# FFT filter and PReLU MLP on one core: the inverse transform's middle array laid out the other way, table and filter loads reordered

## The chip, the cores and the metric

The kernel runs on one core of a Trainium2 chip. The metric is the device time of one execution in microseconds; lower is better. Before the change the median of three runs is 773.36 us.

## The reference

Two computations follow each other. First each of 8 batches of 3008 positions by 256 channels is filtered in the frequency domain along the positions; then all 24064 rows go through a two-layer MLP whose activation has a learned slope for negative values.

```
X = np.fft.rfft(x, axis=1)                      # x: (8, 3008, 256)
Y = X * (filt_r + 1j * filt_i)[None]
y = np.fft.irfft(Y, n=3008, axis=1).reshape(24064, 256)
h = y @ w_in                                    # (256, 2048)
g = np.maximum(h, 0) + alpha * np.minimum(h, 0)
out = g @ w_out                                 # (2048, 256)
```

All inputs and the output are float32. The kernel works in float16 with float32 accumulation.

## The kernel before

**The transform.** 3008 = 94 x 32, so a transform over the positions is done as matrix products: a 94-point transform (stage a), a turn of the array, a 32-point transform with the twiddle factors folded into its tables (piece_b), the product with the filter, then the inverse 32-point transform (piece_c), a second turn, and the inverse 94-point transform (`inverse`), whose result goes to yT, the transposed input of the MLP.

**Batch 0 and the others.** Batches 1 to 7 turn their arrays through DRAM (a_dram, v_dram), hidden beside the MLP of earlier batches. Batch 0 has nothing to hide behind. Its class `First` keeps everything on the chip: it turns by matmuls with the identity matrix `id16` as the moving operand and the array as the weights. The change touches only batch 0's code, the order of loads around it, and the first MLP block.

**Batch 0 in order.** (1) Eight pieces `piece_a` (L322): 94-point transform of 4 of the 32 columns each, evicted to `am`; pieces 0 to 5 are evicted whole by ACT or DVE in turn, pieces 6 and 7 half by ACT and half by DVE (L336). Between them stand `warm` matmuls (L436), which compute nothing that is used. (2) `turn_at` (L338) turns `am` into `at`, two or four of 24 rows at a time. (3) Twelve steps kp: `piece_b(kp)` (matmuls L355, then on DVE the product with the filter, L360, into uu) and `piece_c(kp)` (L363, matmuls L382). PE issues piece_b(kp+2) ahead of piece_c(kp). `piece_c` uses two tables, twi_s and its swapped and sign-scaled copy twx_s; the two halves e=0 and e=1 of the array's rows run at the same time and go to different accumulator tiles. After every second kp `keep_c` (L386) evicts two tiles with ACT into `v` (seen as `vm`). (4) The second turn: `turn` (L393), by `half_t` (two of the 32 columns s, both channel halves) and `piece_t` (four). Its weights are 96 elements of `vm`. (5) `half_d` and `pair_d`: the inverse 94-point transform (L283, constants wi3_s) of four or eight columns, evicted to yT.

In `vm` an element's place is given by (g, m, e), where the column is s = 4g + e and m is the row; a weight load of one column therefore takes every fourth element:

```
m = self.vm.rearrange("p (g m e) -> p g m e", m=96, e=4)                     # L394
nc.tensor.matmul(..., m[:, 8 * f + s // 4, :, s % 4], id16, ...)             # L399
```

**Tables, filter and constants.** The forward table twf_s comes in three parts of 8 of 24 rows (`table`, L416, on SP's DMA queue). A memset on DVE ahead of parts 2 and 3 (L445, L453) holds each load back until DVE has come to that place. `inverse_table` (L419) turns each part into twi_s, and `swapped` (L426) makes twx_s from it, for rows 0 to 7 on DVE, for the others on POOL. The filter comes in three parts of eight DMAs each, issued by POOL (`load_filt`, L132, L140), after the eight loads of x. POOL's DMAs use eight semaphores in turn, so each issue waits until the eighth one before it has landed.

**After batch 0.** The first MLP block (512 rows) runs in halves of 256 rows: `up4` (L563) takes four of the 16 hidden groups, with two accumulating matmuls each (kt = 0 and 1, the two channel halves, L569). Its first call also issues two evictions of the second turn (`later`) and the transposed slopes. From then on a plan written out by hand (`put`, `plan_fft`) lays the pieces of the other batches between the MLP's matmuls; the order of each engine is fixed. In that plan batch 0 still has half_t(6) and (7) at step 3, piece_t(2) at step 1, piece_t(4), (5) at steps 19 and 23, piece_t(6), (7) at 32 and 34, with their pair_d after them.

**Pools.** psH has two tiles of two PSUM banks (hps), psF one of two banks, psO two of one bank (op). `bank("o")`, `bank("h")` and `bank("f")` take one bank from them.

Of the kernel before, what the change touches and what calls it, by code (L numbers as in the profile page):

```python
# [14 lines left out]
N1 = 94  # L15
# [10 lines left out]
def _build_consts():  # L26

    n1, n2, p = np.arange(N1), np.arange(N2), np.arange(32)
    k1 = (2 * (np.arange(NK) // 2) + 24 * (np.arange(NK) % 2))[None, :] + np.arange(2)[:, None]
    k2 = np.where(p < 16, p, 47 - p)  # L30
    g = np.where(p < 16, 1.0, -1.0)

    a1 = 2 * np.pi * n1[:, None, None] * k1[None] / N1
    wf1 = np.stack([np.cos(a1), -np.sin(a1)], axis=2)
    scale = np.where((k1 == 0) | (k1 == 47), 1.0, 2.0)[None, :, None, :] / NFFT
    wi3 = (wf1 * scale).reshape(N1, 96).T
    wfx = wf1.transpose(0, 3, 1, 2).reshape(N1, 96)
# [10 lines left out]
    return wf1, wfx, wfq, wi3, twf  # L48


@with_exitstack
def kernel(
# [8 lines left out]
    out: bass.AP,  # L61
):
    nc = tc.nc
    names = ("wf1", "wfx", "wfq", "wi3", "twf")
# [22 lines left out]
    wfq_s = konst.tile([128, 64], FP16, name="wfq_s")  # L87
    wfx_s = konst.tile([N1, 96], FP16, name="wfx_s")
    wi3_s = konst.tile([96, N1], FP16, name="wi3_s")
    twf_s = konst.tile([128, NK, 64], FP16, name="twf_s")  # L90
    twi_s = konst.tile([128, NK, 64], FP16, name="twi_s")
    filt_s = konst.tile([128, 12, 2, D], FP16, name="filt_s")
# [66 lines left out]
    class Fft:  # L159
        def __init__(self, b):  # L160
            self.b = b
            self.base = (b % 2) * NFFT
            self.uw = {}

        def start_a(self):
# [114 lines left out]
        def inverse(self, pd, g, dh, mh):  # L280
            ps = pd[:, 0 : 4 * N1].rearrange("p (m x) -> p m x", m=4)
            for m in range(4):
                nc.tensor.matmul(ps[:, m], self.zt[:, 8 * g + 4 * mh + m, dh * 128 : dh * 128 + 128],  # L283
                                 wi3_s, start=True, stop=True)
            return ps

        def half_d(self, i, evict, kind, fill=0):
# [19 lines left out]
    def on_dve(o, i):  # L307
        nc.vector.tensor_copy(o, i)  # L308
# [4 lines left out]
    class First(Fft):  # L313
# [7 lines left out]

        def piece_a(self, i, wide):  # L322
            c, sh = i // 2, i % 2
            ps = banks(wide)
            for f in range(2):
                for u in range(4):
                    o = (4 * sh + u) * D + 128 * f
                    nc.tensor.matmul(ps[:, f, 96 * u : 96 * u + 96], xc[(0, c)][0:N1, o : o + 128], wfx_s,
                                     start=True, stop=True)
            o = self.am.rearrange("p (f m s) -> p f m s", f=2, s=N2)[:, :, :, 4 * i : 4 * i + 4]  # L330
            s = ps[:, :, 0:384].rearrange("p f (s m) -> p f m s", s=4)
            if i < 6:
                both[i % 2](o, s)
            else:
                for f in range(2):
                    both[f](o[:, f], s[:, f])  # L336

        def turn_at(self, kp, n, evict, wide=False):  # L338
            ps = banks(wide)
# [23 lines left out]
        def piece_c(self, kp):  # L363
            if kp % 2 == 0 and kp < 10:
                self.ops = [psO.tile([128, 2, D], FP32, name="op") for _ in range(2)]
            if kp == 10:
                pf = banks(False)
                self.ops = [pf[:, e].rearrange("p (k d) -> p k d", k=2) for e in range(2)]
            if kp == 11:
                pf = [bank(kind) for kind in ("h", "o")]  # L370
                self.ops = [t.rearrange("p (k d) -> p k d", k=2) for t in pf]
            kb = 0 if kp > 9 else kp % 2
            u = self.uw.pop(kp)
            tw, tx = (t.rearrange("p k (c g e) -> p k g c e", c=2, e=4) for t in (twi_s, twx_s))
            for par in range(2):
                for f in range(2):
                    for i, t in enumerate((tw, tx)):
                        for e in range(2):
                            r = slice(64 * e, 64 * e + 64)
                            o = self.ops[e][:, kb].rearrange("p (g w) -> p g w", g=16)  # L380
                            o = o[:, 8 * f : 8 * f + 8, 8 * par : 8 * par + 8]
                            nc.tensor.matmul(o.rearrange("p g (c e) -> p g c e", c=2),  # L382
                                             u[r, par, i, 128 * f : 128 * f + 128], t[r, 2 * kp + par],
                                             start=(i == 0), stop=(i == 1))

        def keep_c(self, kp, evicts, n=2):  # L386
            vm = self.vm.rearrange("p (g q k e) -> p g q k e", q=4, k=NK, e=4)
            for e in range(2):
                k = 2 * kp + e
                evicts[e](vm[:, :, :, k : k + 2 * n - 1 : 2],  # L390
                          self.ops[e][:, 0:n].rearrange("p k (g q e) -> p g q k e", q=4, e=4))

        def turn(self, pt, i, n):  # L393
            m = self.vm.rearrange("p (g m e) -> p g m e", m=96, e=4)  # L394
            for u in range(n):
                for f in range(2):
                    o = 256 * (u % 2) + 128 * f
                    s = n * i + u
                    nc.tensor.matmul(pt[0:96, u // 2, o : o + 128], m[:, 8 * f + s // 4, :, s % 4], id16,  # L399
                                     start=True, stop=True)  # L400

        def half_t(self, i, kind):
            pt = bank(kind).unsqueeze(1)
# [38 lines left out]
    for i in range(8):  # L442
        f0.piece_a(i, i % 3 < 2)
        if i == 3:
            nc.vector.memset(twf_s[:, 8:16, 0:1], 0.0)  # L445
            table(8, 16)
            inverse_table(0, bank("o"))
            swapped(0, nc.vector)
            warm(3, bank("o"))
        elif i % 2 == 1:  # L450
            warm((8, 0, 6, 0)[i // 2], bank("o"))
        if i == 5:
            nc.vector.memset(twf_s[:, 16:24, 0:1], 0.0)  # L453
# [17 lines left out]
    nc.sync.dma_start(out=wi3_s, in_=consts["wi3"].ap())  # L471
# [4 lines left out]
    for r in (slice(0, 64), slice(64, 128)):  # L476
        nc.sync.dma_start(out=wfq_s[r], in_=consts["wfq"].ap()[r])
    for kp in range(12):
        if 0 < kp < 10:
            f0.piece_b(kp + 2)  # L480
        if kp == 4:
            nc.vector.memset(win_s[:, :, 0:1], 0.0)
            for kt in range(2):
                nc.gpsimd.dma_start(out=win_s[:, kt], in_=moe_w_in[kt * 128 : (kt + 1) * 128])
            xc[(1, 0)] = load_x(1, 0)
            for q in range(2):
                nc.gpsimd.dma_start(
                    out=wout_s[:, 8 * q : 8 * q + 8],
                    in_=moe_w_out[1024 * q : 1024 * q + 1024].rearrange("(j p) d -> p j d", p=128))
            for c in range(1, 4):  # L490
                xc[(1, c)] = load_x(1, c)
# [44 lines left out]
    class Block:  # L536
# [227 lines left out]
```

## Time and profile before

| what | us |
|---|---|
| median of 3 runs (lowest, highest) | 773.36 (772.82, 773.37) |
| the profiled execution | 772.3 |
| its span | 770.5 |
| PE busy | 760.9 (99%) |
| DVE busy | 634.2 (82%) |
| ACT busy | 583.2 (76%) |
| POOL busy | 147.9 (19%) |
| first product with the filter (L360) begins | 16.84 |
| first matmul of the MLP (L569) begins | 34.20 |

The profile is one execution seen by the hardware profiler; its span runs from the first to the last instruction. PE is TensorE's matmuls and PEld its weight loads, which overlap them; DVE is VectorE, ACT ScalarE, POOL GpSimd, SP SyncE. A row such as `x8 [0.49 <-DMA ...]` tells how many instructions were merged, and in brackets how long the engine was idle before them and what ended that. Matmul durations include the way through the array; what a stream of them costs is seen from one start to the next. Line numbers are those of the kernel before.

### The profile page before, as it was taken

The numbers are of one execution on the slowest core, as the hardware profiler recorded it, in microseconds if no ns is written. First come the engines' busy times: TensorE is split into PE (matmuls) and PEld (weight loads), VectorE is DVE, ScalarE is ACT, GpSimd is POOL, SyncE is SP. The second block draws the span as 40 slices with busy tenths as digits, with TensorE's granted clock in tenths as the row PEclk, the third lists the DMA queues.
The fourth block names the chain that finished last, engine by engine and source line by source line (L and its number), as shares of the span: only waits on it lengthen the run. The fifth ranks groups of instructions, "written<-read, shape, count | busy, mean of one in ns | idle before, by whom it ended". The sixth has DMA issues, their size and how long they took to land.

```text
span 770.5 us, 16598 instructions
## 1 busy us (share of the span) xinstructions
PE 760.9 (99%) x6550; PEld 510.2 (66%) x6550; DVE 634.2 (82%) x1160; ACT 583.2 (76%) x671; POOL 147.9 (19%) x278
## 2 busy tenths in 40 slices
PE   8999999999999999999999999999999999999998
PEld 4666657666666666666666666766666666766666
DVE  4888885889889998899988998999877888666663
ACT  4787788888778787887778777787767777776663
POOL 7620560132211212121201222022101212000000
PEclk9999999999999999999999999999999999999999
DMA  9995797664954558633883538644473223510111
GB/s 162 148 239 156 134 208 195 171 164 119 200 138 94 138 126 169 185 83 94 188 213 89 124 98 177 182 99 117 119 160 98 68 72 96 152 36 28 42 42 56
DMA packets 96814, 99.77 MB, mean 129 GB/s; under 512 B 12020, under 2 KB 83076, under 8 KB 96544
## 3 DMA queue, kind: packets, MB, share of 16 engines
q1 hardware_dynamic: 82048, 69.22, 32.7%
q0 software_dynamic: 14688, 29.49, 21.4%
q8 instruction: 51, 0.84, 0.5%
q14 instruction: 27, 0.22, 0.1%
HBM read 54.74 MB, written 46.66 MB: 132 GB/s over the span
## 4 chain that ended last, share of the span: by engine, by line
PE 96%; ACT 3%; issue 0%; DVE 0%; DMA 0%; ACTq 0%
PE op L600 42%; PE hps L546 41%; PE psF L283 3%; PE hps L261 2%; PE psF L230 1%; PE hps L176 1%; PE op L438 1%; PE hps L202 1%; ACT asb L305 1%; PE hps L569 1%; ACT v L305 1%; PE op L382 1%; PE psF L399 0%; ACT gtb L577 0%; ACT gtb L555 0%; PE hps L355 0%
## 5 line engine op out<-in xcount | busy, mean ns | idle before, releaser
L555 ACT ACTIVATE gtb<-hps 128x1024 f16<-128x1024 f32 (+1 forms) x376 | 377.4, 1006 | 134.7 <-PE hps L546 131.6
L600 PE MATMUL op<-wout_s,gtb 128*128 128x256 f16 x3008 | 431.4, 273 | 0.0
L546 PE MATMUL hps<-yT,win_s 128*128 128x512 f16 (+1 forms) x1504 | 418.4, 375 | 0.9 <-ACT asb L305 0.5
L600 PEld LDWEIGHTS <-gtb 128*128 128x128 f16 x3008 | 290.8, 98 | 164.5 <-issue 11.0
L558 DVE TENSOR_SCALAR m<-gtb,alm_s 128x512 f16<-128x512 f16 (+1 forms) x752 | 227.2, 346 | 98.4 <-ACT gtb L555 96.9
L560 DVE TENSOR_TENSOR gtb<-gtb,m 128x2048 f16<-128x2048 f16 (+1 forms) x188 | 226.1, 1203 | 10.7 <-DVE m L558 0.5
L546 PEld LDWEIGHTS <-win_s 128*128 128x128 f16 x1504 | 142.5, 98 | 55.2 <-issue 6.6
L244 POOL DMA_DIRECT2D sw<-ww x144 | 71.6, 505 | 414.6 <-DVE ww L237 408.8
L605 ACT ACTIVATE osb<-op 128x512 f32<-128x512 f32 (+1 forms) x97 | 56.6, 584 | 12.6 <-PE op L600 11.5
L305 ACT ACTIVATE asb<-hps 128x1024 f16<-128x1024 f32 (+1 forms) x56 | 56.6, 1020 | 5.6 <-PE hps L176 4.3
L305 ACT ACTIVATE v<-hps 128x1024 f16<-128x1024 f32 (+1 forms) x43 | 43.4, 1010 | 10.8 <-PE hps L261 10.6
L237 DVE TENSOR_TENSOR ww<-psF,filts_s 128x1024 f16<-128x1024 f32 x42 | 51.1, 1218 | 0.2 <-PE psF L230 0.2
L238 DVE TENSOR_TENSOR uu<-psF,filt_s 128x1024 f16<-128x1024 f32 x42 | 51.0, 1214 | 0.0
L305 ACT ACTIVATE yT<-psF 128x752 f16<-128x752 f32 x58 | 46.1, 796 | 2.0 <-PE psF L283 1.9
L283 PEld LDWEIGHTS <-zt 96*128 96x128 f16 x512 | 28.6, 98 | 6.3 <-issue 0.6
L283 PE MATMUL psF<-wi_s,zt 96*128 96x94 f16 x496 | 31.0, 205 | 0.3 <-DVE yT L308 0.2
L249 DVE TENSOR_TENSOR uu<-uu,sw 128x1024 f16<-128x1024 f16 x36 | 24.6, 683 | 1.7 <-DMA sw<-ww 1.3
L242 POOL DMA_DIRECT2D uu<-ww x24 | 19.5, 1238 | 33.0 <-DVE uu L238 24.9
L118 POOL DMA_DIRECT2D xs<-in_x_dram x32 | 21.6, 889 | 13.0 <-PE hps L546 4.9
L186 DVE TENSOR_TENSOR xs<-xs 47x2048 f16<-47x2048 f16 x16 | 19.5, 1220 | 0.4
L190 DVE TENSOR_TENSOR xs<-xs 47x2048 f16<-47x2048 f16 x16 | 19.3, 1209 | 0.0
L261 PE MATMUL hps<-uu,twi_s 64*64 64x256 f16 x336 | 17.3, 281 | 0.0
(86 smaller groups left out, 264.2 us busy)
## 6 DMA issues: line engine op xcount, KB each, us to landing
out_dram<-osb SPq DMA_DIRECT2D x128, 128.0 KB
v_dram<-v SPq DMA_DIRECT2D x84, 128.0 KB
zt<-v_dram SPq DMA_DIRECT2D x28, 384.0 KB
sw<-ww POOLq DMA_DIRECT2D x144, 64.0 KB, 2.8
xs<-in_x_dram POOLq DMA_DIRECT2D x44, 192.0 KB, 6.3
at<-a_dram SPq DMA_DIRECT2D x40, 192.0 KB
a_dram<-asb SPq DMA_DIRECT2D x32, 192.0 KB
a_dram<-asb SPq DMA_DIRECT2D x12, 384.0 KB
```

The source lines that it names most:

```text
L237: nc.vector.tensor_mul(ww, px, fs)
L238: nc.vector.tensor_mul(uu, px, f)
L244: nc.gpsimd.dma_start(out=sw[o : o + 32], in_=ww[i : i + 32])
L261: nc.tensor.matmul(ps[64 * par : 64 * par + 64, e, 256 * h : 256 * h + 256], twi_s[r, 4 * q + 2 * h + par], u[r, par, h], start=True, stop ...
L283: nc.tensor.matmul(ps[:, m], self.zt[:, 8 * g + 4 * mh + m, dh * 128 : dh * 128 + 128], wi3_s, start=True, stop=True)
L305: nc.scalar.activation(o, i, AF.Copy)
L546: nc.tensor.matmul(self.hps[:, j % 2, 0:tn], win_s[:, kt, j * 128 : (j + 1) * 128], yT[:, kt, self.t0 : self.t0 + tn], start=(kt == 0), st ...
L555: nc.scalar.activation(g[:, 2 * i : 2 * i + 2], self.hps[:, :, 0:tn], AF.Copy)
L558: nc.vector.tensor_scalar(m[:, 2 * i + h], g[:, 2 * i + h], 0.0, a, OP.min, OP.mult)
L560: nc.vector.tensor_add(g, g, m)
L600: nc.tensor.matmul(self.op[:, si - s0], self.gts[k][:, 128 * si : 128 * si + 128], wout_s[:, k], start=(si == s0 and k == 0), stop=(si == ...
L605: nc.scalar.activation(osb[:, 0:m], self.op[:, 0:m], AF.Copy)
```

## The change

**Layout.** `vm` is now ordered (channel half f, column s, row m), so the 96 weights of one column are contiguous, and the row index is (k, q) and not (q, k). To get there, `piece_c` writes each accumulator tile with its columns in the order (s, q): within a matmul, successive columns go to addresses four floats apart. The table is read as before, in runs of four elements. Since the rows of batch 0's array have another order, its inverse transform has constants of its own, `wif`, loaded beside wi3.

**First outputs.** half_t(0) and half_t(1) become `side_t(0)` and `side_t(1)`: all four columns of one channel half each, so that half_d(0) needs only the first and half_d(2) only the second. ACT and DVE change places in these four evictions. `up4` runs its four kt=0 matmuls ahead of its four kt=1 matmuls.

**Order of loads and small edits.** Table part 2 is loaded after piece 5 (it was after piece 3) and part 3 after piece 7 (after piece 5). The scaling of rows 8 to 15 on POOL stands behind all eight loads of the third filter part, where it stood between its fourth and fifth. Pieces 6 and 7 put their two halves into tiles of their own. Three warm matmuls stand ahead of the turns, not five. wfq comes in one DMA, and wi3 last. The loads of w_in and what follows them are issued at kp 3, not 4.

```
 class First(Fft): piece_a
-            ps = banks(wide)
+            if i < 6:
+                ps = banks(wide)
+                pf = [ps[:, f] for f in range(2)]
+            else:
+                pf = [bank("oh"[i - 6]) for f in range(2)]
...
 class First(Fft): piece_c
-                            o = self.ops[e][:, kb].rearrange("p (g w) -> p g w", g=16)
-                            o = o[:, 8 * f : 8 * f + 8, 8 * par : 8 * par + 8]
-                            nc.tensor.matmul(o.rearrange("p g (c e) -> p g c e", c=2),
+                            o = self.ops[e][:, kb].rearrange("p (g e q) -> p g q e", g=16, q=4)
+                            nc.tensor.matmul(o[:, 8 * f : 8 * f + 8, 2 * par : 2 * par + 2],
                                              u[r, par, i, 128 * f : 128 * f + 128], t[r, 2 * kp + par],
                                              start=(i == 0), stop=(i == 1))
 
         def keep_c(self, kp, evicts, n=2):
-            vm = self.vm.rearrange("p (g q k e) -> p g q k e", q=4, k=NK, e=4)
+            vm = self.vm.rearrange("p (s k q) -> p s k q", q=4, k=NK)
             for e in range(2):
                 k = 2 * kp + e
-                evicts[e](vm[:, :, :, k : k + 2 * n - 1 : 2],
-                          self.ops[e][:, 0:n].rearrange("p k (g q e) -> p g q k e", q=4, e=4))
+                evicts[e](vm[:, :, k : k + 2 * n - 1 : 2],
+                          self.ops[e][:, 0:n].rearrange("p k (s q) -> p s k q", q=4))
 
         def turn(self, pt, i, n):
-            m = self.vm.rearrange("p (g m e) -> p g m e", m=96, e=4)
+            m = self.vm.rearrange("p (f s m) -> p f s m", f=2, m=96)
...
-                    nc.tensor.matmul(pt[0:96, u // 2, o : o + 128], m[:, 8 * f + s // 4, :, s % 4], id16,
+                    nc.tensor.matmul(pt[0:96, u // 2, o : o + 128], m[:, f, n * i + u], id16,
+
+        def side_t(self, f):
+            pt = bank("o")
+            for u in range(4):
+                nc.tensor.matmul(pt[0:96, 128 * u : 128 * u + 128],
+                                 self.vm.rearrange("p (f s m) -> p f s m", f=2, m=96)[:, f, u], id16,
+                                 start=True, stop=True)
+            return self.zt[:, 0:4, 128 * f : 128 * f + 128], pt[0:96].rearrange("p (s d) -> p s d", s=4)
...
     for i in range(8):
         f0.piece_a(i, i % 3 < 2)
         if i == 3:
-            nc.vector.memset(twf_s[:, 8:16, 0:1], 0.0)
-            table(8, 16)
...
-        if i == 5:
-            nc.vector.memset(twf_s[:, 16:24, 0:1], 0.0)
-            table(16, 24)
+        if i in (5, 7):
+            ka = 4 * i - 12
+            nc.vector.memset(twf_s[:, ka : ka + 8, 0:1], 0.0)
+            table(ka, ka + 8)
     load_filt(nc.gpsimd, filt_s, 4, 8)
-    warm(5, bank("o"))
+    warm(3, bank("o"))
...
-    load_filt(nc.gpsimd, filt_s, 8, 12, (0,))
+    load_filt(nc.gpsimd, filt_s, 8, 12)
     swapped(8, nc.gpsimd)
-    load_filt(nc.gpsimd, filt_s, 8, 12, (1,))
...
-        if kp == 4:
+        if kp == 3:
             nc.vector.memset(win_s[:, :, 0:1], 0.0)
...
-    on_dve(*f0.half_t(0, "o"))
-    on_act(*f0.half_t(1, "o"))
+    on_act(*f0.side_t(0))
+    on_dve(*f0.side_t(1))
     later = [f0.half_t(2, "h"), f0.half_t(3, "f")]
-    f0.half_d(0, on_act, "o")
-    f0.half_d(2, on_dve, "o")
+    f0.half_d(0, on_dve, "o")
+    f0.half_d(2, on_act, "o")
...
         def up4(self, i, half, mid):
-            for h in range(4):
-                j = 4 * i + h
-                for kt in range(2):
+            for kt in range(2):
+                for h in range(4):
+                    j = 4 * i + h
                     nc.tensor.matmul(ps[:, h], win_s[:, kt, j * 128 : (j + 1) * 128], yT[:, kt, t],
-                                     start=(kt == 0), stop=(kt == 1))
+                                     start=(kt == 0 and h % 2 == 0), stop=(kt == 1 and h % 2 == 1))
```

Two more edits are left out of this listing: `inverse` takes its constants from `self.wi`, which is wif_s for batch 0 and wi3_s for the others, and the constant `wif` is wi3 with its rows in the new order.

More of the change, by code (lines that the diff above doesn't have):

```diff
@@ L36, in _build_consts @@
     wi3 = (wf1 * scale).reshape(N1, 96).T
+    wif = (wf1 * scale).transpose(3, 1, 2, 0).reshape(96, N1)
     wfx = wf1.transpose(0, 3, 1, 2).reshape(N1, 96)
@@ L47, in _build_consts @@
     twf = fwd.transpose(3, 0, 2, 4, 1, 5).reshape(128, NK, 64)
-    return wf1, wfx, wfq, wi3, twf
+    return wf1, wfx, wfq, wi3, wif, twf
 @with_exitstack
@@ L63 @@
     nc = tc.nc
-    names = ("wf1", "wfx", "wfq", "wi3", "twf")
+    names = ("wf1", "wfx", "wfq", "wi3", "wif", "twf")
     consts = {n: nc.inline_tensor(np.ascontiguousarray(v).astype(np.float16), name="c_" + n)
@@ L89 @@
     wi3_s = konst.tile([96, N1], FP16, name="wi3_s")
+    wif_s = konst.tile([96, N1], FP16, name="wif_s")
     twf_s = konst.tile([128, NK, 64], FP16, name="twf_s")
@@ L162, in __init__ @@
             self.base = (b % 2) * NFFT
+            self.wi = wi3_s if b else wif_s
             self.uw = {}
@@ L283, in inverse @@
                 nc.tensor.matmul(ps[:, m], self.zt[:, 8 * g + 4 * mh + m, dh * 128 : dh * 128 + 128],
-                                 wi3_s, start=True, stop=True)
+                                 self.wi, start=True, stop=True)
             return ps
@@ L327, in piece_a @@
                     o = (4 * sh + u) * D + 128 * f
-                    nc.tensor.matmul(ps[:, f, 96 * u : 96 * u + 96], xc[(0, c)][0:N1, o : o + 128], wfx_s,
+                    nc.tensor.matmul(pf[f][:, 96 * u : 96 * u + 96], xc[(0, c)][0:N1, o : o + 128], wfx_s,
                                      start=True, stop=True)
             o = self.am.rearrange("p (f m s) -> p f m s", f=2, s=N2)[:, :, :, 4 * i : 4 * i + 4]
-            s = ps[:, :, 0:384].rearrange("p f (s m) -> p f m s", s=4)
             if i < 6:
-                both[i % 2](o, s)
+                both[i % 2](o, ps[:, :, 0:384].rearrange("p f (s m) -> p f m s", s=4))
             else:
                 for f in range(2):
-                    both[f](o[:, f], s[:, f])
+                    both[f](o[:, f], pf[f][:, 0:384].rearrange("p (s m) -> p m s", s=4))
         def turn_at(self, kp, n, evict, wide=False):
@@ L397, in turn @@
                     o = 256 * (u % 2) + 128 * f
-                    s = n * i + u
-                    nc.tensor.matmul(pt[0:96, u // 2, o : o + 128], m[:, 8 * f + s // 4, :, s % 4], id16,
+                    nc.tensor.matmul(pt[0:96, u // 2, o : o + 128], m[:, f, n * i + u], id16,
                                      start=True, stop=True)
+        def side_t(self, f):
[5 more added lines that the diff above has]
+            return self.zt[:, 0:4, 128 * f : 128 * f + 128], pt[0:96].rearrange("p (s d) -> p s d", s=4)
         def half_t(self, i, kind):
@@ L470 @@
     f0.turn_at(4, 2, on_act)
-    nc.sync.dma_start(out=wi3_s, in_=consts["wi3"].ap())
+    nc.sync.dma_start(out=wif_s, in_=consts["wif"].ap())
     nc.sync.dma_start(out=al16, in_=moe_alpha.rearrange("(j p) -> j p", p=128))
@@ L475 @@
         nc.sync.dma_start(out=wf1_s[r], in_=consts["wf1"].ap()[r])
-    for r in (slice(0, 64), slice(64, 128)):
-        nc.sync.dma_start(out=wfq_s[r], in_=consts["wfq"].ap()[r])
+    nc.sync.dma_start(out=wfq_s, in_=consts["wfq"].ap())
+    nc.sync.dma_start(out=wi3_s, in_=consts["wi3"].ap())
     for kp in range(12):
```

## The prediction

> **What bounds it now.** I read the page first (busy shares, chain), then a table of stretches, then the timeline and the chain of waits in the first 75 us, because every edit lies there.
>
> ```profile
> PE 760.9 (99%) x6550; PEld 510.2 (66%) x6550; DVE 634.2 (82%) x1160; ACT 583.2 (76%) x671; POOL 147.9 (19%) x278
> PE 96%; ACT 3%; issue 0%; DVE 0%; DMA 0%; ACTq 0%
> ```
>
> PE carries the chain. From about 47 us on its order is fixed and dense, so a microsecond won before then is kept to the end. The stretches (span; busy us and instructions of PE, PEld, DVE, ACT, POOL; clock; DMA share; GB/s) show who limits where:
>
> ```profile
> 16.84:30.68 13.84, 12.62 (x400) 7.86 (x397) 13.78 (x13) 11.04 (x17) 12.53 (x21) 1.00 0.81 118
> 30.68:34.20 3.52, 3.10 (x47) 2.41 (x44) 1.48 (x3) 2.14 (x7) 0.51 (x1) 1.00 1.05 208
> 47.15:60.00 12.85, 12.85 (x96) 8.97 (x96) 12.71 (x24) 10.40 (x12) 2.05 (x4) 1.00 0.96 233
> ```
>
> Between 16.84 and 30.68 DVE is never idle: the twelve filter products (L360) run back to back. From 30.68 to 34.20 it is a chain of short steps. In 47 to 60 both PE and DVE are full.
>
> The timeline shows what starts the products, and the work whose price is in dispute:
>
> ```profile
> 13.98 1.02 DVE L308 CAST gtb<-hps 128x384 f16<-128x384 f32 x2 [1.16 <-ACT gtb L305]
> 16.84 9.16 DVE L360 TENSOR_TENSOR uu<-hps,filt_s 128x1024 f16<-128x1024 f32 x8 [0.49 <-DMA filt_s<-in_filt_r_dram]
> 19.99 0.19 PE L382 MATMUL op<-twi_s,uu 64*128 64x64 f16 x2
> 20.02 0.19 PE L382 MATMUL op<-gtb,uu 64*128 64x64 f16 x2
> 20.58 0.48 POOL L429 TENSOR_SCALAR gtb<-twi_s,signs_s 128x256 f16<-128x256 f16 x1
> 21.01 2.12 POOL L140 DMA_DIRECT2D filt_s<-in_filt_i_dram  x4
> ```
>
> The first product waits for the filter. Pairs of L382 start 0.03 us apart. Beside the products runs a loop on PE and ACT, here as the chain of waits gives it:
>
> ```profile
> 24.74 1.08 ACT v L305 x2
> 25.82 0.04 issue
> 25.87 0.39 PE op L382 x15
> 26.26 0.34 PE hps L355 x16
> 26.60 0.39 PE op L382 x16
> ```
>
> One turn (eviction of v, c step, b step, c step) is 1.08 + 0.04 + 0.39 + 0.34 + 0.39 = 2.24 us, and DVE needs 2 x 1.145 = 2.29 us for the same two steps. The loop is only 0.05 us from being the bound.
>
> Last, the weight loads by line (ns min/median/max), and the price of eight turns on the later chain:
>
> ```profile
> L399 PEld LDWEIGHTS <-v x64: 163/186/188, 31.8 to 68.2; 128*96 128x96 f16 x64
> L176 PEld LDWEIGHTS <-wf_s x48: 119/123/126, 44.9 to 180.0; 94*96 94x96 f16 x48
> 49.92 0.68 PE psF L399 x8
> 57.80 0.34 PE psF L283 x8
> ```
>
> **Term 1, start of the products: 0.2 us gained.** The two DVE copies of pieces 6 and 7 (13.98 to 15.01) waited for ACT, since both read one tile; with a tile each they can start when their four matmuls end, near 13.45. The turns follow 0.5 us sooner and piece_b(0) ends near 15.95, not 16.50. But the product waits for the eighth filter piece, issued at 12.72 and landed at 16.72. Its packets move from 14.25 to 15.7, beside table part 3, which was issued at 12.85 behind the memset after piece 5. In the new order part 2 takes exactly that place, and part 3 follows after piece 7's copy, near 14.5. So one table part still runs beside the piece; only the small constant loads leave. The two warming matmuls that go (0.43 us) stood before the turns, where PE waits for the copies anyway, and the granted clock is 1.00 in every stretch. I take 0.2, with 0 (nothing changes) and 0.5 (PE's own gain) as ends.
>
> **The products themselves: unchanged at 12 x 1.145 us.** Covers that this needs: (a) the scaling of table rows 8 to 15 on POOL moves behind four filter issues of 2.12 us. It ended at 21.06 and piece_c(4) reads it at about 23.4; it will end near 23.15. Two microseconds of cover shrink to 0.25; without it c waits up to 0.4 us. (b) Table part 3 lands near 17.2, and inverse_table(16), due near 17, may hold PE some tenths; piece_b(2) behind it waits for product 0 (18.06) anyway. (c) SP's six small constants move behind the later memset: first use is beyond 33 us. (d) The w_in issue needs the memset one product earlier and follows the second scaling: 24.6 in place of 25.18, so its second half lands near 33.4 in place of 34.04; it is needed near 33.8 to 34. Each at nothing.
>
> **Term 2, last product to first MLP step: 0.58 us.** Before, L569 starts 3.52 us after the last product ends (34.20 less 30.68), its kt=1 half waits for the second yT, and the next PE work comes 4.61 us after the product. After: the turn starts as before 1.10 us behind it, but a matmul each 55 ns instead of 90 (term 3); four turns of one half end at 1.49, ACT evicts to 2.12 (0.59), the inverse ends at 2.51, DVE evicts (0.55) to 3.10, L569 starts at 3.15. Its kt=0 half needs only this yT; the other is ready at 3.35. Eight at 0.109 end at 4.02: 4.61 less 4.02 is 0.59.
>
> **Term 3, the turns: 0.77 us.** L399 starts a matmul each 90 ns, as its loads are 90 ns apart. L343, with the same 128 moving columns and contiguous weights, starts one each 55 ns. That the stride does it I read from L176: 96 contiguous columns load in 123 ns, where the first, unqueued L399 load takes 163; 90 less 40 is 50, under the 55 of the matmul. Eight turns fall from 0.68 to 0.44. Where this counts: piece_t(2), 0.24; half_t(6) and (7), nothing, as DVE's evictions (36.88 to 39.35) end last there; piece_t(4) and (5), 0.05, because DVE has no gap from 43.17 to 61.28 and the inverse at 57.65 waits for its eviction that ends at 57.60; piece_t(6) and (7), 2 x 0.24. Ends: 0 and 1.3.
>
> The Trainium skill, "TensorE: Matmul & The Clock Gate", section "LDWEIGHTS (loading the stationary operand)", gives a load as columns over 1.2 ns, an estimate of 80 ns for 96 columns whatever their stride. By it the whole sum would be about 0.8 us; this trace differs, with loads of 32, 64 and 96 contiguous columns at 88, 107 and 123 ns, half a nanosecond a column.
>
> **Term 4, the scattered columns: taken at 0.** L382 now writes runs of eight columns and starts a pair each 29 ns for 64 columns; afterwards no two successive columns are neighbours. No row has PE writing lone columns. The near end is L382 itself (runs of eight with gaps run at full rate); the far end comes from ACT's reads of PSUM: 752 lone elements take 0.80 us and 376 take 0.48, 0.84 ns each, so 64 would take 54 ns. I take the same instruction's row, and carry 54 as a rival.
>
> **Sum.** 0.2 + 0.58 + 0.77 = 1.55 us. The profiled execution took 772.3 us (span 770.5), 1.06 below the median 773.36 of the three runs; it becomes 770.75, the median 771.8.
>
> **Rivals.** *Scattered columns at 54 ns a pair.* Each c step grows by 8 x 25 ns = 0.2, the loop from 2.24 to 2.64, above DVE's 2.29. About ten of the twelve c steps are then exposed: 2.0 us lost, +0.45 in all, 773.8. For it: nothing in the trace shows PSUM giving one lone element in less than 0.84 ns. Against: gaps cost L382 nothing now. The Trainium skill, "PSUM — Partial Sum Buffer", section "Specifications (TRN2)", says that any non-contiguous pattern slows matmuls significantly; L382's present gaps at 29 ns do not agree, its lone columns no run here shows yet.
>
> *Slower: the accumulation reads and writes each lone column, 2 x 54 = 108 ns a pair.* Same place; ten steps of 8 x 79 ns cost 6.3 us: 778.1. It decides from about 68 ns a pair, where the loss is 3.1 us and the end is 0.2% above before.
>
> *The change doesn't do what it says: the load's length is set by its 96 columns, not by the stride.* Term 3 falls away, and of term 2 only the earlier kt=0 start, 0.2, is left: with 0.2 for term 1 and 0.05 elsewhere 0.45 us, 772.9. L176 speaks against it.
>
> **How the numbers follow.** Forecast 0.55, 54 ns 0.25, 108 ns 0.10, load unchanged 0.10. This kernel's measurement tells about 0.2%, 1.55 us, from no change, and the forecast sits on that edge: of its 0.55 I put 0.33 on faster and 0.22 on same. The 54 ns case is 0.18 same, 0.06 slower, 0.01 faster (a pair nearer 40 ns); the 108 ns case slower; the load case 0.01 faster, 0.05 same and, with a late POOL scaling or filter on top, 0.04 slower. Rounded: faster 0.35, same 0.45, slower 0.20. The range: 770.6 is all best ends of terms 1 to 3 (0.5 + 0.7 + 1.3 = 2.5) less 0.26, half the spread of the three runs; 774.8 leaves out the 108 ns case and the worst tail of the 54 ns case. The forecast's own range is 770.6 to 772.8.
>
> **What would show it.** In the page after: L399's loads near 120 ns and eight turns in 0.44 us (term 3); pairs of L382 0.03 us apart (0.05 or more is the rival) and the loop at 2.24; the first product between 16.3 and 16.85, waiting for the filter; the products without a gap; L569 3.15 us after the last of them. A wait of piece_c(4) for POOL, or a gap between products, would make it wrong.

## The result and the profile after

The changed kernel is slower: 774.31 us, median of 21 runs (773.30 to 775.80), against 772.85 (772.34 to 776.33) for the kernel before, measured beside it; the ratio is 1.0016, 95% interval 1.0009 to 1.0023, so 0.7 to 1.8 us (0.2%). The profiled execution took 773.98 us, its span is 772.2. Line numbers of the changed kernel are shifted: L360 became L366 (product), L382 L387 (piece_c), L305 L308 (ACT's evictions), L308 L311 (DVE's), L399 L403 (turn) and L409 (side_t), L421 L433 (the matmuls of inverse_table), L569 L579 (first MLP block), L546 L556 (the MLP behind it).

The page's shares have hardly moved, but the chain of waits now holds DVE, ACT and 1% DMA:

```profile
PE 761.2 (99%) x6548; PEld 509.5 (66%) x6548; DVE 634.5 (82%) x1160; ACT 583.5 (76%) x671; POOL 148.0 (19%) x278
PE 94%; DVE 3%; ACT 2%; DMA 1%; issue 0%; ACTq 0%
```

The table of stretches, here the one that held the products of the kernel before (columns as there). DVE's busy time falls from 13.78 to 12.09 us: it now waits between products.

```profile
16.84:30.68 13.84, 11.51 (x337) 7.55 (x323) 12.09 (x12) 9.97 (x15) 12.60 (x22) 1.00 0.85 129
```

The timeline shows both ends of the trouble. The first product starts earlier (16.05, before 16.84), but PE then stands 1.37 us for part 3 of the table, and the third product 0.88 us for PE. The matmul pairs of L387 take 0.25 us each (before 0.19) and their starts are 0.05 to 0.06 us apart, not 0.03.

```profile
16.05 2.36 DVE L366 TENSOR_TENSOR uu<-hps,filt_s 128x1024 f16<-128x1024 f32 x2 [0.21 <-PE hps L361]
18.47 0.40 PE L433 MATMUL op<-ids,twf_s 128*128 128x128 f16 x4 [1.37 <-DMA twf_s<-c_twf]
19.29 1.22 DVE L366 TENSOR_TENSOR uu<-hps,filt_s 128x1024 f16<-128x1024 f32 x1 [0.88 <-PE hps L361]
19.80 0.25 PE L387 MATMUL op<-twi_s,uu 64*128 64x64 f16 x2
19.85 0.25 PE L387 MATMUL op<-gtb,uu 64*128 64x64 f16 x2
```

The chain of waits, in order of time: first the table part, then one turn of the loop.

```profile
14.57 3.86 DMA twf_s<-c_twf
...
23.93 1.08 ACT v L308 x2
25.01 0.04 issue
25.05 0.60 PE op L387 x15
25.65 0.34 PE hps L361 x16
26.00 0.60 PE op L387 x16
26.59 1.08 ACT v L308 x2
```

The turn takes 26.59 - 23.93 = 2.66 us, before 2.24: two c steps of 0.60 for 0.39. It is longer than DVE's 2.29, so every second product waits 0.22 us, and the last one 0.85 (before 0.06).

The turns did what the change set out to do (weight loads, ns, and eight turns on the chain):

```profile
L403 PEld LDWEIGHTS <-v x56: 120/123/125, 35.1 to 69.9; 128*96 128x96 f16 x56
67.54 0.45 PE psF L403 x8
```

**Where the time went**, from the two traces: products start -0.79 us; products themselves 17.12 us for 13.84, +3.28; last product to first MLP matmul 3.60 for 3.52, +0.08; from there to the 65th matmul of the MLP's first layer (the first of L556) 12.49 for 12.95, -0.46; from that to the end of the span 722.94 for 723.35, -0.41. Sum +1.70, the difference of the spans.

### The profile page after: what moved, and what is told of

The parts are those of the page before. It is cut to its first block, busy times and chain, and to the rows that moved or that the text cites. A ratio compares the mean times of both kernels' runs of the same rounds, so it can differ in the third digit from the quotient of the medians.

```text
span 772.2 us, 16594 instructions
## 1 busy us (share of the span) xinstructions
PE 761.2 (99%) x6548; PEld 509.5 (66%) x6548; DVE 634.5 (82%) x1160; ACT 583.5 (76%) x671; POOL 148.0 (19%) x278
## 4 chain that ended last, share of the span: by engine, by line
PE 94%; DVE 3%; ACT 2%; DMA 1%; issue 0%; ACTq 0%
PE op L610 42%; PE hps L556 41%; PE psF L286 3%; PE hps L264 2%; PE psF L233 1%; PE op L450 1%; PE hps L179 1%; PE hps L205 1%; PE op L387 1%; DVE gtb L593 1%; DVE zt L311 1%; ACT asb L308 1%; DVE m L592 1%; ACT v L308 1%; DMA twf_s<-c_twf 0%; ACT gtb L565 0%
## 5 line engine op out<-in xcount | busy, mean ns | idle before, releaser
L556 PE MATMUL hps<-yT,win_s 128*128 128x512 f16 (+1 forms) x1504 | 418.4, 375 | 0.9 <-ACT asb L308 0.3
L556 PEld LDWEIGHTS <-win_s 128*128 128x128 f16 x1504 | 142.4, 98 | 55.2 <-issue 6.1
L308 ACT ACTIVATE asb<-hps 128x1024 f16<-128x1024 f32 (+1 forms) x56 | 56.6, 1020 | 5.6 <-PE hps L179 4.3
L308 ACT ACTIVATE v<-hps 128x1024 f16<-128x1024 f32 (+1 forms) x43 | 43.5, 1011 | 10.7 <-PE hps L264 10.6
L308 ACT ACTIVATE yT<-psF 128x752 f16<-128x752 f32 x58 | 46.1, 795 | 2.0 <-PE psF L286 1.9
L286 PE MATMUL psF<-wi_s,zt 96*128 96x94 f16 x448 | 27.9, 205 | 0.1
```

What stands on the lines that cost most here:

```text
L308: nc.scalar.activation(o, i, AF.Copy)
L556: nc.tensor.matmul(self.hps[:, j % 2, 0:tn], win_s[:, kt, j * 128 : (j + 1) * 128], yT[:, kt, self.t0 : self.t0 + tn], start=(kt == 0), st ...
```

## The experiments

Two explanations stood against each other. The first: accumulator columns without a neighbour are written at half rate, so the loop of PE and ACT passes DVE and is the bound. The rival: the columns cost little, and it is the later table part that holds up piece_b and with it everything behind. Single profiles of one kernel differ in where the products start by some tenths of a microsecond, so medians and ratios to the kernel before decide, and a trace is read for distances within it.

### Which part costs what

**Table loads back in their old places, the rest of the change kept.**

```
         if i == 3:
+            nc.vector.memset(twf_s[:, 8:16, 0:1], 0.0)
+            table(8, 16)
...
-        if i in (5, 7):
+        if i == 5:          # part 3 here, nothing after piece 7
```

> The changed kernel with the table loads back at their old places (part 2 behind piece 3, part 3 behind piece 5); all else as changed. Theory A (two losses: scattered columns in the c steps, and table part 3 landing at 18.4 so that PE stands 1.4 us ahead of inverse_table(16) and DVE 0.9 us ahead of its third product): the wait for the table goes, the third product follows without a gap, and about 0.9 us come back: near 773.4 where the changed kernel has 774.3. Theory B (the scattered columns alone; the loop on PE and ACT, at 2.67 us a turn, sets the end whatever the table does): unchanged within 0.2, since the loop would only start earlier by what the filter then costs. In both the pairs of L382's successor stay 56 ns apart.

Measured: 772.77 us (11 runs; before 772.92), ratio 0.9997 (0.9988 to 1.0006). PE no longer waits for the table (inverse_table(16) at 17.73, before the first two products are done), and the gaps of 0.22 and the 0.85 stay, as do the 0.60 of the c step. So in the changed kernel the later loads cost 774.31 - 772.77 = 1.5 us, more than the 0.88 us gap. The two traces show less of it, 0.40 us (the last product ends at 33.17 there, at 32.77 here): single executions of one kernel differ by more than that.

**Old layout, the rest kept** (later table loads included).

```
-    o = self.ops[e][:, kb].rearrange("p (g e q) -> p g q e", g=16, q=4)
-    nc.tensor.matmul(o[:, 8*f : 8*f + 8, 2*par : 2*par + 2],
+    o = self.ops[e][:, kb].rearrange("p (g w) -> p g w", g=16)
+    o = o[:, 8*f : 8*f + 8, 8*par : 8*par + 8]
+    nc.tensor.matmul(o.rearrange("p g (c e) -> p g c e", c=2),
...            # keep_c, turn, side_t and the constants wi3_s as before
```

> The changed kernel with the old layout of the turned array (accumulators in runs of eight, weights every fourth element, wi3 for all batches); table loads, side_t, up4's order and the rest as changed. Theory A: pairs 29 ns apart again, the loop at 2.24 hidden under the products, loads of the turn 90 ns apart again; the table wait stays. The products start 0.8 earlier than before the change and lose 0.9 at the gap; with 0.2 from up4's order the time is that of before within 0.3: 772.6 to 773.0. Theory C (the table loads are the main loss): it stays slower than before by 0.8 or more.

Measured: 773.68 us (11 runs), ratio 1.0002 (0.9993 to 1.0011). The loop's gaps of 0.22 are gone, the pairs are 29 ns apart at full clock and the turns 89 ns. But part 3, issued at 14.42, took 4.27 us, PE waited until 18.74, and the products had gaps of 1.06, 0.24 and 0.85 us. The last of these falls in a stretch in which PE itself ran slower: the b step that this product reads ended at 23.02, and its filter had landed by 20.5. Columns as in the table of stretches, and the granted clock is third from the end:

```profile
15.00:20.00 5.00, 3.19 (x76) 1.89 (x76) 3.50 (x4) 2.49 (x4) 4.27 (x9) 1.00 1.08 162
20.00:25.00 5.00, 5.00 (x145) 3.24 (x144) 3.91 (x4) 3.71 (x6) 4.88 (x9) 0.66 0.75 98
```

After the wait PE got 0.66 of its clock for 5 us, and the c steps took 0.54 us there, 0.38 later. So here the wait cost more than its own length. How often it does is not shown. Of the changed kernel's 21 executions the five with a mean clock of 0.998 or less took 775.1 to 775.8 us, the other sixteen 773.3 to 774.83; but of the 98 executions of the kernel before that were measured beside the experiments, 16 have such a clock too, without a late table. The median of the sixteen is 774.08, so the clock explains about 0.2 of the 1.5 us.

**Only the later table loads**, added to the kernel before.

```
-            nc.vector.memset(twf_s[:, 8:16, 0:1], 0.0)    # after piece 3
-            table(8, 16)
...
-        if i == 5:
+        if i in (5, 7):
```

> The kernel before with the table loads of the changed one (part 2 behind piece 5, part 3 behind piece 7), nothing else. Theory A (late tables are a loss by themselves): the filter lands near 15.9 and the products start near 16.5, but inverse_table(16) waits for part 3 until about 18.4; the third product and the loop on PE and ACT start about 0.6 to 1.0 later than before, so 773.4 to 773.9. Theory B (they only hurt a loop that the scattered columns have already made the bound): with pairs at 29 ns the loop catches up under the products and the time is 772.7 to 773.0.

Measured: 773.53 us (11 runs; before 772.94), ratio 1.0005 (0.9997 to 1.0014). Part 3 was issued at 15.39 and took 3.27 us, so inverse_table(16) ran at 18.71. But the products started late as well here (17.26), and the gaps are only 0.01 and 0.15. PE's wait is 0.78 us, where it was 1.37 in the changed kernel. On its own the edit costs about half a microsecond, which can't be told from nothing.

**Only the small edits** (two tiles for pieces 6 and 7, less warming, scalings behind the filter, order of side_t and of kt); layout and table loads as before. The diff to the changed kernel is that of the first and the second experiment taken together:

```
+            table(8, 16)                                   # after piece 3
...
-    o = self.ops[e][:, kb].rearrange("p (g e q) -> p g q e", g=16, q=4)
+    o = self.ops[e][:, kb].rearrange("p (g w) -> p g w", g=16)
```

> The changed kernel with both the old layout and the old table times: what is left is side_t, up4's order, the separate tiles of pieces 6 and 7, the earlier w_in load, the scaling behind the filter loads and the fewer warm matmuls. Both theories: a small gain, 0.2 to 0.5 us from the earlier first MLP step: 772.3 to 772.7. Slower than 772.9 would mean that one of them costs something that I have not seen.

Measured: 772.36 us (11 runs), ratio 0.9994 (0.9985 to 1.0003); products from 16.23 on with one gap, 0.30 ahead of the last. It comes from POOL: the scaling of table rows 8 to 15, now behind the filter loads, ended at 23.37, and PE waited 0.32 us for it in piece_c(4) (23.42). Of the 0.61 us by which the products start sooner, 0.22 is left at their end (30.46, before 30.68); the first MLP matmul starts 3.54 us after that, the 65th 12.83 us behind the first (before 12.95).

**Only the layout**, added to the kernel before.

```
-    o = self.ops[e][:, kb].rearrange("p (g w) -> p g w", g=16)
+    o = self.ops[e][:, kb].rearrange("p (g e q) -> p g q e", g=16, q=4)
...
-    m = self.vm.rearrange("p (g m e) -> p g m e", m=96, e=4)
+    m = self.vm.rearrange("p (f s m) -> p f s m", f=2, m=96)
```

> The kernel before with the scattered layout alone (piece_c, keep_c, turn, wif), tables and all else as before. The prediction's rival gave this mechanism 2.0 us lost on the loop against about 1.1 won by the turns, so 773.7. If the turns win more than the loop loses: below 772.6. Pairs 56 ns and turns 56 ns apart in both.

Measured: 774.45 us (11 runs), ratio 1.0015 (1.0007 to 1.0024). Pairs 56 ns apart, turns 56 ns, the loop 2.67 us (ACT's evictions of v start at 20.32, 22.99, 25.66, 28.33). So the layout alone makes a loss as large as the whole change: by the ratios it is +1.2 us, the tables +0.4 and the small edits -0.5, in sum +1.1, where the whole change measured 0.0016 x 772.85 = +1.2. That the sum fits says less than it seems, since each part is known to about 0.7 us either way. Layout and small edits together, the first experiment, measured -0.2 and not +0.7; and taken out of the changed kernel, the later loads are worth 1.5 us by the medians and the layout 0.6. The parts don't simply add.

### What in the layout costs, and what it gives

The layout does two things at once. The next two kernels do one each. Each leaves out the matching edits of the other steps, so the second turn takes elements that belong to other rows and columns, and batch 0's result is not that of the reference; the amount of work is the same.

**Lone accumulator columns alone** (evictions and turns as before).

```
-    o = self.ops[e][:, kb].rearrange("p (g w) -> p g w", g=16)
-    o = o[:, 8*f : 8*f + 8, 8*par : 8*par + 8]
-    nc.tensor.matmul(o.rearrange("p g (c e) -> p g c e", c=2),
+    o = self.ops[e][:, kb].rearrange("p (g e q) -> p g q e", g=16, q=4)
+    nc.tensor.matmul(o[:, 8*f : 8*f + 8, 2*par : 2*par + 2],
```

> The kernel before, with only the order of the accumulators' columns in the c steps as in the changed kernel (lone columns, four floats apart); evictions and turns as before, so batch 0's columns are permuted in the output. It prices term 4 by itself. Theory A (pairs 56 ns apart, the loop on PE and ACT at 2.67 us a turn and above DVE's 2.29): 1.7 to 2.2 us above before, 774.6 to 775.1. If PE had room for it beside the products: within 0.3 of before.

Measured: 774.78 us (12 runs; before 773.01), ratio 1.0020 (1.0011 to 1.0029), +1.77 by the medians. The chain of waits has the same loop:

```profile
23.44 1.08 ACT v L305 x2
24.52 0.04 issue
24.57 0.60 PE op L381 x15
25.17 0.34 PE hps L355 x16
25.51 0.60 PE op L381 x16
26.11 1.08 ACT v L305 x2
```

The products take 15.65 us, 1.81 more than before, and the first MLP matmul comes 3.96 us after the last of them, 0.44 more, since the last two c steps write lone columns as well. That is 2.25 us in this execution, 1.77 by the medians and 1.55 by the ratio, and it comes from nothing but where PE writes.

**Contiguous weights alone** (the accumulators and v as before, the turn reads 96 successive elements).

```
-    m = self.vm.rearrange("p (g m e) -> p g m e", m=96, e=4)
+    m = self.vm.rearrange("p (f s m) -> p f s m", f=2, m=96)
...
-    nc.tensor.matmul(..., m[:, 8*f + s // 4, :, s % 4], id16, ...)
+    nc.tensor.matmul(..., m[:, f, s], id16, ...)
```

> The kernel before, with only the turn's weight reads as in the changed kernel (96 neighbours, not every fourth element); accumulators and evictions as before, so batch 0's columns are permuted in the output. It prices term 3 and the turns' part of term 2 by themselves: 0.77 for the later turns and about 0.3 to 0.4 ahead of the first MLP step, 1.1 in all: 771.8. If loads were bound by their 96 columns: 772.8.

Measured: 772.24 us (12 runs), ratio 0.9986 (0.9978 to 0.9995). The loads (the turns are 56 ns apart; c steps 0.39 and the loop 2.24 as before):

```profile
L399 PEld LDWEIGHTS <-v x64: 119/123/125, 32.0 to 67.5; 128*96 128x96 f16 x64
```

The first MLP matmul comes 3.24 us after the last product (0.28 sooner), the 65th is 12.62 us behind the first (0.33 less), and the rest of the span is 722.93 (0.42 less): 1.03 us, where the ratio gives 1.08 and the medians 0.77. The gain is real; the lone columns cost 1.55 and 1.77 by the same two measures.

### How many neighbours a column needs

**Runs of two, in the kernel before**: v, accumulators and table have e=2 in place of e=4. The weights then take every second element, the accumulators stay in runs (four, with gaps), and the table is read in twos.

```
-    tw, tx = (t.rearrange("p k (c g e) -> p k g c e", c=2, e=4) for t in (twi_s, twx_s))
+    tw, tx = (t.rearrange("p k (c g e) -> p k g c e", c=2, e=2) for t in (twi_s, twx_s))
...
-    o = o[:, 8*f : 8*f + 8, 8*par : 8*par + 8]
+    o = o[:, 16*f : 16*f + 16, 4*par : 4*par + 4]
```

> The kernel before with its layout's run length changed from four to two, nothing else: the accumulators are written in runs of four, the table is read in runs of two, the weights of a turn are every second element. If neighbouring pairs are what a fast write needs, pairs stay 29 ns apart; if runs of two of the table are read at full rate too, nothing is lost in the c steps. If a weight load needs more than two elements in 16 bytes, the turns go from 90 towards 55 ns: then the sum is about 0.8 for the later turns and 0.3 for the first ones less, near 771.7. If the loads stay at 90: 772.85.

Measured: 772.49 us (11 runs; before 772.92), ratio 0.9995 (0.9986 to 1.0004). Its loads, and its chain of waits:

```profile
L399 PEld LDWEIGHTS <-v x64: 122/124/126, 33.1 to 68.6; 128*96 128x96 f16 x64
```

```profile
21.02 1.08 ACT v L305 x2
22.10 0.04 issue
22.14 0.44 PE op L382 x15
22.58 0.34 PE hps L355 x16
22.92 0.43 PE op L382 x16
23.36 1.08 ACT v L305 x2
```

Every second element loads as fast as contiguous ones, and the turns follow each other at 56 ns. But the pairs are 36 ns apart, not 29, and the loop of 23.36 - 21.02 = 2.34 us passes DVE's 2.29; the last product waits 0.45. By the medians 0.43 us is won, about half of the 0.77 that the turns alone gave.

**Runs of one** (e=1): contiguous weights, accumulators in twos, table read one element at a time, and ACT's eviction reads lone floats from PSUM and writes lone elements of v.

```
-    tw, tx = (t.rearrange("p k (c g e) -> p k g c e", c=2, e=4) for t in (twi_s, twx_s))
+    tw, tx = (t.rearrange("p k (c g e) -> p k g c e", c=2, e=1) for t in (twi_s, twx_s))
...
-    o = o[:, 8*f : 8*f + 8, 8*par : 8*par + 8]
+    o = o[:, 32*f : 32*f + 32, 2*par : 2*par + 2]
```

> As runs of two, with a run length of one: accumulators in runs of two, the table read element by element, weights contiguous. Weight loads as in the changed kernel (turns 55 ns apart), which is worth about 1.1 us. If lone columns, and not gaps, slow the write, pairs stay near 29 ns as far as the write goes; reading the table one element at a time is the open price: at 29 ns a pair 771.7, at 56 ns a pair 2.0 us are lost on the loop and it ends near 773.7.

Measured: 787.78 us (4 runs), ratio 1.0189 (1.0173 to 1.0205). ACT's timeline has what made it so; 512 lone elements per partition take about 1.4 us, where they took 0.60:

```profile
30.29 2.52 ACT L305 ACTIVATE v<-op 128x512 f16<-128x512 f32 x2 [1.06 <-PE op L382]
```

The loop became 4.43 us (0.2 of it because PE's clock was granted at 0.50 from 26 to 41 us, with b steps of 0.56 for 0.34). The pairs are 62 ns apart, at the full clock as at the half, with accumulators in twos: reading the moving table one element at a time costs PE a little more than writing lone columns.

**Accumulators in runs of two, table in twos, v as in the runs of two**: this differs from that kernel only in the length of the accumulators' runs.

```
-    o = self.ops[e][:, kb].rearrange("p (g w) -> p g w", g=32)
-    o = o[:, 16*f : 16*f + 16, 4*par : 4*par + 4]
+    o = self.ops[e][:, kb].rearrange("p (g c r e) -> p r g c e", g=32, c=2, r=2)
+    o = o[:, par, 16*f : 16*f + 16]
```

> As the layout with a run length of two, but the accumulators' row order exchanged so that a matmul writes runs of two columns where that one wrote runs of four (batch 0's constants in the matching order). One question: how far apart its pairs start. If two neighbouring columns are enough for a full-rate write: about 33 ns, c steps of 0.44, the time of that run, 772.5. If the write needs four or more neighbours: 40 to 56 ns and 773.5 or more.

Measured: 772.97 us (8 runs; before 773.01), ratio 0.9996 (0.9986 to 1.0007). Matmuls of L384 (ns min, median, max; below them those of runs of four) and the loop, 2.34 us, have not changed:

```profile
L384 PE MATMUL op<-twi_s,uu x84: 191/196/201, 19.3 to 31.6; 64*128 64x64 f16 x84
L382 PE MATMUL op<-twi_s,uu x84: 191/197/201, 19.7 to 32.1; 64*128 64x64 f16 x84
```

So a column with one neighbour is written as fast as one in a run of four, and it is the lone ones that cost (tried at one distance only, four floats). The 36 ns of the pairs stay as they are when the accumulators' runs go from four to two, so the 7 ns more than before lie most likely in reading the table by twos; no run has one without the other.

### A version that beats both

**The changed kernel with runs of two and the table loads in their old places.**

```
+            table(8, 16)                                   # after piece 3
...
-    o = self.ops[e][:, kb].rearrange("p (g e q) -> p g q e", g=16, q=4)
-    nc.tensor.matmul(o[:, 8*f : 8*f + 8, 2*par : 2*par + 2],
+    o = self.ops[e][:, kb].rearrange("p (g w) -> p g w", g=32)
+    o = o[:, 16*f : 16*f + 16, 4*par : 4*par + 4]
```

> The small edits and the old table times, with the layout's run length of two (accumulators in runs of four, table in runs of two, weights every second element). The run of the kernel before with this layout had turns 56 ns apart and c steps of 0.44 us in place of 0.39, the loop at 2.34. With the small edits the turns' gain of about 0.8 later and 0.5 before the first MLP step stands against 0.3 to 0.6 lost on the loop: 771.8 to 772.2, faster than both kernels. If the loop's loss eats it: 772.5.

Measured: 771.75 us (12 runs; before 772.94), ratio 0.9985 (0.9977 to 0.9993). Products from 16.42, the loop 2.34, the last product still 0.44 us late, first L580 matmul 3.45 us after it.

**The same with one warming less.** The last product waited for piece_b(11), which stood in PE's queue behind two warming matmuls.

```
-        if 7 < kp < 10:
+        if kp == 9:
             warm(2, banks(False)[:, 0])
```

> The run that joined the small edits, the old table times and the run length of two, with the two warm matmuls behind piece_c(8) taken out. They stand ahead of piece_b(11), whose product began after a gap of 0.44 us there. If that gap is theirs, the last product and all behind it come 0.3 to 0.45 sooner: 771.3 to 771.5. If PE's clock drops for want of them, or the wait for ACT's eviction takes their place: 771.7 or more.

Measured: 771.30 us (11 runs, 770.95 to 771.74; before 773.01), ratio 0.9973 (0.9965 to 0.9982): by the medians 1.7 us, by the ratio 2.1 us faster than the kernel before, and the best of all. The gap ahead of the last product is gone. In its profiled execution another opened, 0.76 us ahead of the eighth product, and the chain of waits names POOL's scaling of table rows 8 to 15:

```profile
22.18 0.59 ACT v L308
22.77 0.02 issue
22.80 0.95 POOL gtb L441
23.75 0.47 POOL gtb L442
24.21 0.04 issue
24.25 0.42 PE op L388 x14
```

POOL had stood 1.21 us ahead of a filter issue and came that much later. So there may be more to have here; a kernel with these scalings back ahead of the filter loads was not run.

## Why the prediction was wrong

The forecast was 771.8 us, faster by 1.55; the change measured 774.31 us and is slower. That this lies in the range given is due to the rival, which the range took in.

**Term 4 failed, and with it the sum.** The price of lone columns was taken from the nearest row, 29 ns a pair, with 54 ns as a rival. It is 56 ns, and the kernel that has this alone lost 1.77 us. The rival had its mechanism and its size right: loop 2.64 (2.66 measured), 2.0 us. L382's runs of eight were not near to lone columns: what decides is whether a column has a neighbour, and the row had no case without one. ACT's 0.84 ns for a lone PSUM element, the far end, gave the figure almost exactly; that reads by one engine and writes by another agree so well may be chance, and no run shows a common cause. The 108 ns case did not come.

The Trainium skill, "PSUM — Partial Sum Buffer", section "Specifications (TRN2)", which says that any non-contiguous pattern slows matmuls significantly, pointed the right way. By the runs it is too broad: runs of eight, four and two with gaps take 29 to 36 ns a pair, lone columns 56.

**Cover (b) of term 1 failed too.** It let part 3 land near 17.2, with inverse_table(16) held by tenths. The issue was forecast right (14.5, it was 14.57), but the load took 3.86 us beside the filter, and 3.27 and 4.27 in two other kernels: PE stood 1.37 us. The step put no price on a late load; by the medians it costs 0.6 us on the kernel before, which is within the noise, and 1.5 in the changed one. Why it costs more together with the lone columns stays open; the clock is at most a small part of it.

**Term 1 itself was too small.** The six profiled executions with the new order (the changed kernel and five experiments) start the products at 16.30 on average, the eight with the old order (the kernel before and seven experiments) at 17.04: 0.7 us, for which 0.2 with an end of 0.5 was given. It comes with the small edits and not with the later tables (alone: 17.26). The term expected the eighth filter piece to hold it; in the changed kernel the piece landed at 15.92, 2.99 us after its issue where it had taken 4.00, and PE ended last. Which of the edits sped the transfer up was not tested. A sooner start is not all won: the loop or a wait behind it took most of it back in the small edits alone.

**Cover (a) was too thin.** The POOL scaling held in the changed kernel, whose c steps come later (it ended at 23.44, piece_c(4) reads its result at 25.06). With pairs at 29 ns, as forecast, and the tables in their old places PE waited 0.32 us for it (the small edits alone), near the 0.4 that the prediction named for a missed cover; and it was what ended last in the fastest version. The SP constants (cover c) and the w_in load (d, second half at 32.69 for 33.4) cost nothing, as said.

**Term 2 was half right.** The faster turn brings the first MLP matmul 0.28 us nearer where nothing else is changed (3.24, for 3.15 with the new order). In the changed kernel it is 3.60: the last two c steps write lone columns as well, and the turn starts 1.54 us after the last product, not 1.10. The earlier kt=0 half is worth 0.13 (12.49 us to the 65th matmul with it, 12.62 with contiguous weights alone; 12.83 against 12.95 in the small edits alone), for 0.2.

**Term 3 was right** in cause and size. Loads 123 ns, turns 56 ns apart, eight in 0.45 us; of the 0.77 forecast, contiguous weights alone gave 0.33 + 0.42 behind the first MLP matmul. The rival that the load's length doesn't change is out: every fourth element takes 186 ns a load and 90 ns a turn, every second one 124 and 56, contiguous ones 123 and 56. The Trainium skill, "TensorE: Matmul & The Clock Gate", section "LDWEIGHTS (loading the stationary operand)", has a load's time depend on its columns alone, by estimate 80 ns for 96 of them; the runs do not agree. The 0.8 us that the prediction gave by this rule is more than the 0.45 of its own rival with the same assumption, which also takes the faster turns out of term 2.

**The loop's margin** was seen (0.05 us between 2.24 and 2.29) and made to weigh too little. With so little room any step that adds to the c step shows: 7 ns a pair put the loop at 2.34.

## What to carry to other kernels

When an array is laid out for its reader, look at every engine that touches it and for each at its shortest run: here runs of two for PE's writes to PSUM and for ACT's, a stride of two for its weights and runs of two for the moving operand served all of them, at 36 ns a pair for 29, where making one contiguous left another with lone elements. Where a row of the trace is to price an access pattern, ask if it holds the feature that sets the cost (here, a column without a neighbour), and not if it looks alike. A load that is put off behind others is priced by the time that it takes beside them, and the parts of a change that share a bound may cost more together than alone.

## What the runs showed of the hardware that was not expected

- PE writes to PSUM: 64 columns a matmul, pairs 29 ns apart in runs of eight, 36 ns in runs of four or two (with a table read in twos), 56 ns as lone columns four floats apart.
- The moving operand, 16-bit elements: a pair takes 29 ns with runs of four, 36 with runs of two and 62 one at a time (the accumulators' runs are eight, four or two, and two). The 62 ns were the same at a granted clock of 1.00 and of 0.50.
- Weight loads of 96 columns: every second 16-bit element is as fast as contiguous ones, every fourth takes a turn from 56 to 90 ns.
- ACT's eviction of 512 elements from PSUM to 16-bit elements in SBUF: 0.60 us in runs of two or four, 1.34 to 1.45 us one at a time (on both sides; which one costs is not shown); of 256 elements 0.38 us in fours, 0.47 to 0.49 in twos.
- In the kernel with the old layout PE's granted clock was 0.66 over 5 us (0.50 from 21 to 23 us) after a stretch (15 to 20 us) in which PE had been busy for 3.19 of 5 us; the longest wait in it was 1.78 us. In the changed kernel a wait of 1.37 us left the clock at 1.00. The Trainium skill, "TensorE: Matmul & The Clock Gate", Part 1, ties the slower state to an idle window of about 3.4 us; here shorter idle time was enough.
